# A written order for the whole first phase of a packed-attention and mixer kernel, with some copies moved from ScalarE to VectorE

## The chip, the cores and the metric

The kernel runs on one core of a Trainium2 chip. The metric is the device time of one execution in microseconds (us). Several runs of a kernel are summed up by their median. The engines are TensorE (PE in the profile; its weight loads are PEld), VectorE (DVE), ScalarE (ACT), GpSimd (POOL) and SyncE (SP), which here issues nearly all transfers.

## What is computed

The input has 8 batches of 8 heads; q, k and v are 576 x 64 per head, p is 32 x 64.

```python
    p_packed = sm_attn(p, k, v)
    out = sm_attn(q, p_packed, p_packed)
...
    xt = x.transpose(0, 2, 1)
    h = xt @ U @ V
    u = x + h.transpose(0, 2, 1)
    ch = np.maximum(u @ w_ch1, 0.0) @ w_ch2
    return (u + ch).astype(np.float32)
```

`sm_attn` is softmax attention. The first attention packs 576 keys into 32 rows per head, the second spreads them over 576 tokens. Its output, 576 x 512 per batch, goes through a token mixer of rank 32 (U, V) and a channel mixer (512 to 2048 to 512, with a Relu). U, V and the two channel matrices are float64 and are turned into float32 on the chip.

## The kernel before

**Two phases.** The first phase does the packing attention of all 16 units (a unit is a batch and four of its heads), turns the first 12 of 16 pieces of `w1` into float32, prepares U and V, and carries batch 0 through the second attention and the token mixer. The second phase runs the channel mixer over 8 batches: `gemm1` (h_ps, 16 slices per batch) and `gemm2` (o), each product split into three in fp32r from a high and a low part. What is left of the first phase (the last products of units 14 and 15), the next batches' attention and the `w2` conversions are put between these products by hand.

**One unit of the first phase.** `a_load` and `a_load_v` fetch k (tile `kx`, 576 KB, three buffers) and v (`vt`, 576 KB in three transfers, three buffers). `a_turn` transposes k on PE into PSUM (`k_ps`), ten products in three groups, and copies it out (`kT`; lines 276 and 280 on ScalarE, 274 on VectorE for one copy per unit). `a_scores` makes the scores (`s_ps`, one buffer), `a_softmax` takes their maximum on VectorE (line 496) and the exponential on ScalarE (line 498, tile `e`). `a_turn_back` transposes `e` (`m_ps`, lines 295 and 297) and copies it out (`eT`, lines 507 and 510), `a_pack` multiplies it with v (line 526) and scales (`two`), `a_heads` transposes that (line 536) into `ppTa`, which for batches 1 to 7 goes through DRAM (`ppTd`).

**Weights.** `float32_of` takes one ScalarE instruction (lines 79 and 185) and three of VectorE (lines 80 to 82) for each piece of 128 x 512 float64. The raw pieces lie in `bits` and `bits2`, two buffers each, so a load waits for an earlier piece's last VectorE instruction.

**What sets the order.** For the first phase the code loops over the units; a few lists say what is done in each round: `turns` (pieces of `w1`) and `early` (steps of batch 0). Within that phase a scheduler of the language's tile layer puts each engine's instructions into an order, from a model of their times. The second phase is compiled as it is written (`manual_schedule`, line 613). On the chip every engine works through its own list in order, and an instruction whose input is late holds all those behind it on its engine; that goes for SP's transfers too.

Just ahead of the second phase the code starts the loads of batch 1's q (`steps.pop(0)()`, line 602, tile `x`) and of three pieces of `w2` (line 193), and converts the first of these.

Of the kernel before, what the change touches and what calls it, by code (L numbers as in the profile page):

```python
# [20 lines left out]
def packed_attention_mixer_kernel(  # L21
# [51 lines left out]
    def float32_of(x, t, raw, out=None, tested=False):  # L73


        low, high = raw[:, :, 0], raw[:, :, 1]
        out = x if out is None else out.bitcast(I32)
        if not tested:
            nc.scalar.activation(t, high.bitcast(F32), AF.Abs, scale=REBIAS)
        nc.vector.tensor_single_scalar(x, t.bitcast(I32), 3, op=ALU.logical_shift_left)  # L80
        nc.vector.scalar_tensor_tensor(x, high, SIGN, x, op0=ALU.bitwise_and, op1=ALU.bitwise_or)
        nc.vector.scalar_tensor_tensor(out, low, 29, x, op0=ALU.logical_shift_right, op1=ALU.bitwise_or)
        return out.bitcast(F32)
# [86 lines left out]
    order = list(numbered("c" + "".join(plan)))  # L170
# [10 lines left out]
    tests = {}  # L181

    def test_w1(n):
        tests[n] = conv_tile(F32)
        nc.scalar.activation(tests[n], bits["w1", n][:, :, 1].bitcast(F32), AF.Abs, scale=REBIAS)

    def convert_w1(n):
        x, c = chunks[n]
        float32_of(conv_tile(I32), tests.pop(n), bits.pop(("w1", n)), w1t[x][:, QW * c:QW * c + QW], tested=True)
# [13 lines left out]
    def split_w2(kt, x):  # L203
        hi, lo = w2_parts(kt)
        nc.scalar.copy(hi, x)
        nc.vector.tensor_tensor(lo, x, hi.bitcast(F32), op=ALU.subtract)

# [10 lines left out]
    def load_uv():  # L218
        ub = x_tile()[:, :10 * R].bitcast(I32)
# [4 lines left out]
        vbits = x_tile()[:, :S // 2].bitcast(I32)  # L224
        nc.sync.dma_start(out=vbits, in_=V.rearrange("r (q x) -> (r q) x", q=4))
        return ub, vbits

    def prepare_uv(ub, vbits):
        ux = float32_of(conv_tile(I32)[:, :5 * R], conv_tile(F32)[:, :5 * R], ub.rearrange("p (x t) -> p x t", t=2))
        for (n, ks) in ((P, slice(0, 4)), (64, slice(4, 5))):  # L230
            nk = ks.stop - ks.start
            src = ux.rearrange("p (k r) -> p k r", k=5)[:n, ks].unsqueeze(2).to_broadcast([n, nk, 4, R])
            nc.vector.tensor_copy(ua4[:n, ks], src)
            nc.vector.tensor_tensor(ua4[:n, ks, 1], src[:, :, 0], ua4[:n, ks, 0].bitcast(F32), op=ALU.subtract)
        n = I // 2
        w = S // 4
        vq = float32_of(conv_tile(I32)[:, :w], conv_tile(F32)[:, :w], vbits.rearrange("p (x t) -> p x t", t=2))
        spread = x_tile()[:, :4 * P].rearrange("p (q a r) -> p q a r", q=4, a=4)
        nc.gpsimd.tensor_copy(spread, ident.rearrange("p (r q) -> p q r", q=4).unsqueeze(2).to_broadcast([P, 4, 4, R]))
        spread = spread.rearrange("p q a r -> p q (a r)")  # L240
        for hf in range(2):
            v_ps = bank()
            for y in range(2):
                nc.tensor.matmul(v_ps[:, w * y:w * y + w], lhsT=spread[:, 2 * hf + y], rhs=vq, start=True, stop=True)
            vx = v_ps[:, :2 * w].rearrange("p (i c) -> p i c", c=NT)
            blocks = vx[:, :, :8].rearrange("p i (a k r) -> p r k i a", a=2, k=2)
            ns = slice(n * hf, n * hf + n)
            pairs = [(vs[:, LAST][:, ns], vx[:, :, 8])]
            for r in range(2):
                dst = vs[:, HALF[r].start:HALF[r].start + 4 * I].rearrange("p (k i a) -> p k i a", k=2, a=2)[:, :, ns]  # L250
                pairs.append((dst, blocks[:, r]))
            for dst, src in pairs:
                nc.scalar.copy(dst, src)
                nc.vector.tensor_tensor(dst[96:], src[96:], dst[96:].bitcast(F32), op=ALU.subtract)


# [5 lines left out]
    def turn(t, x, h, bank, split=False):  # L262
# [3 lines left out]
        if h < 2:  # L266
# [3 lines left out]
            src = t_ps.rearrange("p (k a z i) -> p a z k i", k=2, a=2, z=2)  # L270
            for a in range(2):
                dst = t[:, 2 * h:2 * h + 2, :4 * I].rearrange("p z (k i a) -> p a z k i", k=2, a=2)[:, a]
                if a and split:
                    nc.vector.tensor_copy(dst, src[:, a])
                else:
                    nc.scalar.copy(dst, src[:, a])  # L276
        else:
            for h in range(2):
                nc.tensor.transpose(t_ps[:64, P * h:P * h + P], x[:, h, SM:], ident)
            nc.scalar.copy(t[:64, :, LAST], t_ps[:64, :2 * P].rearrange("p (h i) -> p h i", h=4))  # L280
# [21 lines left out]
    def attention(b, res):  # L302
# [11 lines left out]
        def turn_q(g, h):  # L314
            if h == 0:
                st["t", g] = pipe.tile([P, 4, 5 * I], F32, name="xT", bufs=1)
            turn(st["t", g], st["x", g], h, bank)

        def scores_q(g):
            e = st["e", g] = pipe.tile([P, S // 32, 32], F32, name="e", bufs=1)  # L320
            ss = [bank() for _ in range(2)]
# [515 lines left out]
```

## Time and profile before

| | us |
|---|---|
| median of 3 runs (823.89 to 826.15) | 824.42 |
| the profiled execution | 822.64 |
| its span in the profile | 820.9 |
| PE busy in the span | 802.2 (98%) |
| VectorE busy | 353.9 (43%) |
| ScalarE busy | 318.4 (39%) |
| GpSimd busy | 75.5 (9%) |
| transfers | 70.23 MB |

A busy PE is not a PE at its peak, since matmuls overlap and their ends are modelled. The shares are means over both phases. The profile's view by stretches gives the busy time of each engine between two times; the timeline lists instructions in order of time, with the idle time ahead of them and what ended it in brackets; the waits tell who waited for whom (us in total, times, the longest); a group of instructions stands with its count, its busy us and the mean ns of one. PEclk is the clock granted to TensorE as a share of full speed.

### The profile page before, as it was taken

What the parts mean: (1) busy time and instruction counts of PE and PEld (TensorE: products, weight loads), DVE (VectorE), ACT (ScalarE), POOL (GpSimd) and SP (SyncE); (2) the same over time, 40 slices, a digit from 0 to 9 for tenths busy, and PEclk for the clock granted to TensorE, in tenths of its full rate; (3) what the DMA queues carried; (4) which work ended last, traced back from release to release, by engine and by line L of the source; (5) the groups of instructions that cost most, each with busy time, mean ns of one, the idle gap of its engine ahead of it and who ended that gap; (6) DMA issues with size and microseconds to landing.
All of it is one profiled execution on the core that took longest, in us unless ns stands there. A gap on an engine that the chain in (4) does not pass through costs nothing.

```text
span 820.9 us, 15500 instructions
## 1 busy us (share of the span) xinstructions
PE 802.2 (98%) x6272; PEld 645.6 (79%) x6272; DVE 353.9 (43%) x782; ACT 318.4 (39%) x958; POOL 75.5 (9%) x108
## 2 busy tenths in 40 slices
PE   7889999999999999999999999999999999999997
PEld 5556677888888888887888888888888788888886
DVE  3777579973343234333434233333434234332231
ACT  4688765453333232343234232343234232332231
POOL 0122101110011001010101011000101011100000
PEclk8999999999999999999999999999999999999999
DMA  9999774325002120122002210131012200030001
GB/s 298 350 358 320 225 171 132 126 87 155 2 1 97 52 56 1 30 88 73 2 2 96 79 28 1 66 100 27 1 62 84 59 1 2 15 111 2 1 1 64
DMA packets 60310, 70.23 MB, mean 86 GB/s; under 512 B 22864, under 2 KB 41296, under 8 KB 60240
## 3 DMA queue, kind: packets, MB, share of 16 engines
q1 hardware_dynamic: 59920, 68.73, 27.2%
q8 instruction: 49, 0.80, 0.4%
q10 hardware_dynamic: 320, 0.52, 0.2%
q14 instruction: 21, 0.17, 0.1%
HBM read 53.64 MB, written 15.60 MB: 84 GB/s over the span
## 4 chain that ended last, share of the span: by engine, by line
PE 91%; DMA 4%; ACT 2%; DVE 1%; SPq 1%; issue 1%; POOL 0%; ACTq 0%; POOLq 0%
PE o L87 17%; PE o L89 16%; PE o L88 16%; PE h_ps L87 9%; PE h_ps L88 8%; PE h_ps L89 8%; PE t_ps L424 4%; DMA vt<-in_v_dram 2%; PE o L688 2%; PE t_ps L269 2%; DMA kx<-in_k_dram 2%; PE t_ps L289 1%; PE t_ps L367 1%; PE t_ps L295 1%; PE k_ps L269 1%; DMA bits<-in_moe_w_ch_dram 1%
## 5 line engine op out<-in xcount | busy, mean ns | idle before, releaser
L87 PE MATMUL o<-w2h,hh 128*128 128x512 f32 x512 | 206.5, 403 | 0.0
L89 PE MATMUL o<-w2h,hl 128*128 128x512 f32 x512 | 202.4, 395 | 0.0
L88 PE MATMUL o<-w2l,hh 128*128 128x512 f32 x512 | 201.9, 394 | 0.0
L671 DVE SCALAR_TENSOR_TENSOR hl<-h_ps,hh 128x256 fp32r<-128x256 f32 x256 | 105.4, 423 | 199.4 <-ACT hj L670 185.2
L668 ACT ACTIVATE hh<-h_ps 128x256 fp32r<-128x256 f32 x256 | 98.8, 387 | 179.5 <-PE h_ps L89 178.9
L87 PE MATMUL h_ps<-ah,wth 128*128 128x320 f32 (+1 forms) x512 | 157.7, 308 | 0.3 <-DVE hl L671 0.3
L88 PE MATMUL h_ps<-al,wth 128*128 128x320 f32 (+1 forms) x512 | 151.8, 296 | 0.1
L89 PE MATMUL h_ps<-ah,wtl 128*128 128x320 f32 (+1 forms) x512 | 151.4, 296 | 0.0
L87 PEld LDWEIGHTS h_ps<-ah,wth 128*128 128x128 f32 x512 | 96.6, 189 | 25.4 <-issue 20.2
L89 PEld LDWEIGHTS o<-w2h,hl 128*128 128x128 f32 x512 | 96.4, 188 | 22.4
L87 PEld LDWEIGHTS o<-w2h,hh 128*128 128x128 f32 x512 | 96.9, 189 | 21.0 <-issue 4.6
L88 PEld LDWEIGHTS o<-w2l,hh 128*128 128x128 f32 x512 | 97.0, 189 | 16.9
L88 PEld LDWEIGHTS h_ps<-al,wth 128*128 128x128 f32 x512 | 96.8, 189 | 2.4 <-POOL al L387 0.5
L89 PEld LDWEIGHTS h_ps<-ah,wtl 128*128 128x128 f32 x512 | 97.0, 189 | 0.0
L431 DVE TENSOR_TENSOR wtl<-t_ps,wth 128x256 fp32r<-128x256 f32 x128 | 48.5, 419 | 98.6 <-ACT wth L430 95.1
L430 ACT CAST wth<-t_ps 128x256 fp32r<-128x256 f32 x128 | 43.6, 374 | 105.5 <-PE t_ps L424 96.1
L387 POOL TENSOR_TENSOR al<-aT,ah 128x320 fp32r<-128x320 f32 (+1 forms) x32 | 25.7, 806 | 211.3 <-ACT ah L386 211.3
L330 POOL TENSOR_TENSOR e<-e,m 128x576 f32<-128x576 f32 x16 | 18.7, 1170 | 259.2 <-DVE m L329 255.1
L424 PE MATMUL t_ps<-w1t,ppT 64*32 64x512 f32 x512 | 35.9, 601 | 0.0
L276 ACT COPY xT<-t_ps 128x256 f32<-128x256 f32 x64 | 21.3, 392 | 37.5 <-PE t_ps L269 36.7
L386 ACT CAST ah<-aT 128x320 fp32r<-128x320 f32 (+1 forms) x32 | 13.7, 434 | 45.8 <-DVE aT L385 45.7
L670 ACT ACTIVATE hj<-h_ps 128x64 f32<-128x64 f32 x128 | 28.2, 220 | 0.0
(121 smaller groups left out, 824.5 us busy)
## 6 DMA issues: line engine op xcount, KB each, us to landing
bits<-in_moe_w_ch_dram SPq DMA_DIRECT2D x32, 512.0 KB, 4.6
kx<-in_k_dram SPq DMA_DIRECT2D x16, 576.0 KB, 7.0
x<-in_q_dram SPq DMA_DIRECT2D x16, 576.0 KB, 4.9
vt<-in_v_dram SPq DMA_DIRECT2D x32, 256.0 KB, 7.1
out_dram<-bits SPq DMA_DIRECT2D x32, 256.0 KB, 2.4
aD<-aT SPq DMA_DIRECT2D x16, 288.0 KB, 2.1
aP<-aD SPq DMA_DIRECT2D x32, 128.0 KB, 3.6
ppP<-ppD SPq DMA_DIRECT2D x32, 64.0 KB, 3.3
```

The costliest lines, as they stand in the source:

```text
L87: nc.tensor.matmul(ps, lhsT=lh, rhs=rh, start=start, stop=False)
L88: nc.tensor.matmul(ps, lhsT=lh, rhs=rl, start=False, stop=False)
L89: nc.tensor.matmul(ps, lhsT=ll, rhs=rh, start=False, stop=stop)
L269: nc.tensor.transpose(t_ps[:, o:o + P], x[:, h, P * j:P * j + P], ident)
L276: nc.scalar.copy(dst, src[:, a])
L387: nc.gpsimd.tensor_tensor(al[:, g, ns], aT[:, ns], ah[:, g, ns].bitcast(F32), op=ALU.subtract)
L424: nc.tensor.matmul(f_ps[g][xs], lhsT=ppT[b][zs, g, xs], rhs=w1t[h // 2][zs, QW * c:QW * c + QW], start=True, stop=True)
L430: nc.scalar.copy(hi[:, g], f_ps[g][:, cs])
L431: nc.vector.tensor_tensor(lo[:, g], f_ps[g][:, cs], hi[:, g].bitcast(F32), op=ALU.subtract)
L668: nc.scalar.activation(hh[:, ms], src, AF.Relu)
L670: nc.scalar.activation(hj[:, jslot(self.b, kt), self.js], h_ps[:, LAST], AF.Relu)
L671: nc.vector.scalar_tensor_tensor(hl[:, ms], src, 0.0, hh[:, ms].bitcast(F32), op0=ALU.max, op1=ALU.subtract)
```

## The change

The loop over the units is gone. In its place stands a string, `opening`, of 557 words. Each word is one group of instructions of one engine (or one load): `lk` loads k of the next unit, `k0` to `k2` are the three groups of transposes, `k0a` and the like the copies out of them, `s0` to `s2` scores, maximum and exponential, `b0` and `b1` the transposes back, `m0` to `m2` the packing, `h0` to `h2` the heads, `w0` to `w4` one piece of `w1`, `u` and `v` with a digit U and V, `q`, `s3` to `sa`, `t`, `x` and `y` batch 0, `f` the first folded weights, `z` the first piece of `w2`, `qq` the load of batch 1's q. The functions are cut up so that each word has one of its own. `manual_schedule` now begins ahead of this string, so each engine's list in the first phase is the string's order. A `v` at the end of a word (`k1bv`) gives that copy to VectorE instead of ScalarE; 61 words have it. The groups are those of before, with twelve pieces of `w1`, and the second phase's code does what it did.

```diff
-    turns = [0, 0, 1, 1, 0, 2, 0, 2, 1, 0, 2, 1, 0, 2, 0, 0]
-    early = [0, 0, 0, 0, 3, 2, 4, 3, 2, 5, 3, 2, 0, 0, 0, 0]
-    NW1 = sum(turns)
+    opening = (
+        "w0 lk lp lp lv u0 w1 w2 lk w3 lk lv w4 p0 k1 p1 p0 lv k1av k1bv k2 p1v k0 k2av u1 k0bv lk u2 k0av lp u2 s0 "
...
+        "h0 m1 b1a h1v m2 z5 z0 z6 "
+    )
+    NW1 = opening.split().count("w0")
...
+    def copy(scalar):
+        return nc.scalar.copy if scalar else nc.vector.tensor_copy
...
-            for a in range(2):
-                dst = t[:, 2 * h:2 * h + 2, :4 * I].rearrange("p z (k i a) -> p a z k i", k=2, a=2)[:, a]
-                if a and split:
-                    nc.vector.tensor_copy(dst, src[:, a])
-                else:
-                    nc.scalar.copy(dst, src[:, a])
...
+    def turned(t, t_ps, h, a, scalar=True):
+        if h < 2:
+            src = t_ps.rearrange("p (k a z i) -> p a z k i", k=2, a=2, z=2)
+            dst = t[:, 2 * h:2 * h + 2, :4 * I].rearrange("p z (k i a) -> p a z k i", k=2, a=2)[:, a]
+            copy(scalar)(dst, src[:, a])
+        else:
+            copy(scalar)(t[:64, :, LAST], t_ps[:64, :2 * P].rearrange("p (h i) -> p h i", h=4))
...
+    ctx.enter_context(tc.manual_schedule())
...
-    n_w1 = 0
-    for i in range(NU):
-        if i > 0:
-            a_turn_back(i - 1, bank_a("m"))
-        a_scores(i)
-        if i + 1 < NU:
-            a_load_v(i + 1)
-            a_turn(i + 1)
-        if i + 2 < NU:
-            a_load(i + 2)
-        a_softmax(i)
...
+    for word in opening.split():
+        name = word.rstrip("v") if word not in stages else word
+        stage = next(stages[name])
+        if name in either:
+            stage(name == word)
+        else:
+            stage()
...
-    ctx.enter_context(tc.manual_schedule())
```

**SP, near the end of the first phase.** `kx` is k, `vt` is v, `x` is batch 1's q, `bits` from `in_moe_w_ch_dram` with line 193 is `w2`. Before, from the load of the second piece of `w2` on; the last pair of `vt` is unit 13's:

```order
L193 DMA bits<-in_moe_w_ch_dram 128x1024
L542 DMA ppTd_80<-ppTa 128x256
L193 DMA bits<-in_moe_w_ch_dram 128x1024
L258 DMA x<-in_q_dram 128x2x576
L258 DMA kx<-in_k_dram 128x2x576
L465 DMA vt<-in_v_dram 64x4x256 x2
L467 DMA vt<-in_v_dram 64x4x64
L258 DMA x<-in_q_dram 128x2x576
L465 DMA vt<-in_v_dram 64x4x256 x2
L467 DMA vt<-in_v_dram 64x4x64
```

The same place in the changed kernel, from the load of the last k on; line 220 is now the load of `w2`, lines 622 and 624 that of v, line 311 that of k and q. Units 12, 13 and 14 are the three `vt`:

```order
L311 DMA kx<-in_k_dram 128x2x576
L622 DMA vt<-in_v_dram 64x4x256 x2
L624 DMA vt<-in_v_dram 64x4x64
L220 DMA bits<-in_moe_w_ch_dram 128x1024
L622 DMA vt<-in_v_dram 64x4x256 x2
L624 DMA vt<-in_v_dram 64x4x64
L723 DMA ppTd_81<-ppTa 128x256
L622 DMA vt<-in_v_dram 64x4x256 x2
L624 DMA vt<-in_v_dram 64x4x64
L311 DMA x<-in_q_dram 128x2x576 x2
L129 DMA ppT<-ppTd_78 128x256
L220 DMA bits<-in_moe_w_ch_dram 128x1024
```

Both q loads, the load of `ppT` and two of the three `w2` loads have moved behind unit 13's v; one `w2` load, the first, stands ahead of it.

**VectorE, at the start of the program**, behind its first memset. `w1t` is a converted piece of `w1`, `os` the working tiles of a conversion, `x` the raw bits of U, `ua` the spread U, `sm` the first unit's maximum. Before:

```order
L274 COPY kT<-k_ps 128x2x128
L496 TENSOR_REDUCE sm<-s_ps 128x1
L80 TENSOR_SCALAR os<-os 128x512
L274 COPY kT<-k_ps 128x2x128
L81 SCALAR_TENSOR_TENSOR os<-bits_146,os 128x512
```

Now, from the second instruction of the first conversion to the first maximum:

```order
L81 SCALAR_TENSOR_TENSOR os<-bits_138,os 128x512
L82 SCALAR_TENSOR_TENSOR w1t_101<-bits_138,os 128x512
L332 COPY kT<-k_ps 128x2x128 x2
L638 TENSOR_SCALAR pT<-t_ps 128x256
L334 COPY kT<-k_ps 64x4x64
L332 COPY kT<-k_ps 128x2x128
L80 TENSOR_SCALAR os<-os 128x160
L332 COPY kT<-k_ps 128x2x128
L81 SCALAR_TENSOR_TENSOR os<-x,os 128x160
L82 SCALAR_TENSOR_TENSOR os<-x,os 128x160
L273 CAST ua_109<-os 128x512
L658 TENSOR_REDUCE sm<-s_ps 128x1
```

A whole conversion, five copies of `kT`, one of `pT` and the preparation of U now stand ahead of the first maximum, which was VectorE's second instruction there.

**VectorE, at the end of the first phase**, up to the second phase's first `hl`. Before:

```order
L496 TENSOR_REDUCE sm<-s_ps 128x1
L274 COPY kT<-k_ps 128x2x128
L514 RECIPROCAL sm<-sm 128x1
L496 TENSOR_REDUCE sm<-s_ps 128x1
L671 SCALAR_TENSOR_TENSOR hl<-h_ps_1710,hh 128x256
```

Now; `w2l` is the low part of the first piece of `w2`, `aT` batch 0's mixed tokens:

```order
L461 TENSOR_TENSOR aT_1312<-t_ps,aT_1312 128x256
L80 TENSOR_SCALAR os<-os 128x512
L658 TENSOR_REDUCE sm<-s_ps 128x1
L81 SCALAR_TENSOR_TENSOR os<-bits,os 128x512
L687 RECIPROCAL sm<-sm 128x1
L82 SCALAR_TENSOR_TENSOR os<-bits,os 128x512
L718 COPY ppTa<-t_ps 128x128
L239 TENSOR_TENSOR w2l_106<-os,w2h_105 128x512
L866 SCALAR_TENSOR_TENSOR hl<-h_ps_1710,hh 128x256
```

The conversion of the first piece of `w2` has moved from some twenty VectorE instructions earlier to the very end of the phase.

More of the change, by code (lines that the diff above doesn't have):

```diff
@@ L1 @@
 from contextlib import ExitStack
-from itertools import product
+from itertools import count, product
 import concourse.bass as bass
@@ L223, in load_uv, with load_v @@
         nc.sync.dma_start(out=ub[:64, 8 * R:], in_=rows[:, 8])
[L224 to L232, printed above, removed]
+    def load_v():
+        uv["vb"] = x_tile()[:, :S // 2].bitcast(I32)
+        nc.sync.dma_start(out=uv["vb"], in_=V.rearrange("r (q x) -> (r q) x", q=4))
@@ new lines, in step_turn, with step_scores, step_most, step_total @@
+        def step_turn(g, h):
+            turn_q(g, h)
+            for a in range(2 if h < 2 else 1):
+                turned_q(g, h, a)
+        def step_scores(g):
+            scores_q(g)
+            side(g, 0)
+            side(g, 1)
+        def step_most(g):
+            most(g)
+            each(g, "m", ALU.subtract)
+        def step_total(g):
+            for k in range(3):
+                total(g, k)
+            each(g, "s", ALU.mult)
+        def step_tokens(k0):
+            if k0 == 0:
+                room()
+            tokens(k0)
+            split_tokens(k0, False)
+            split_tokens(k0, True)
@@ L747, in convert_late_w1 @@
         n = order.pop(0)[1]
-        test_w1(n)
-        convert_w1(n)
+        begin_w1(n)
+        for _ in range(3):
+            go_w1(n)
         load_next()
```

514 lines of the change are left out of this document (316 added, 198 removed), and 16 rows, old and new, of the table opening.

## The prediction

> **What bounds the kernel now.** I read the page first, then the busy time by stretches, then the matrix engine's timeline for the end of the first phase.
>
> ```profile
> span 820.9 us, 15500 instructions
> ...
> 0.00:20.00 20.00, 15.40 (x109) 11.94 (x110) 5.78 (x11) 9.04 (x23) 1.45 (x11) 0.83 0.93 295
> 20.00:40.00 20.00, 17.11 (x293) 10.45 (x291) 14.26 (x36) 14.33 (x47) 2.46 (x4) 0.92 1.08 351
> 40.00:60.00 20.00, 18.29 (x302) 12.10 (x294) 14.38 (x28) 16.93 (x54) 4.62 (x8) 0.99 1.07 363
> 60.00:80.00 20.00, 17.23 (x269) 11.99 (x271) 16.55 (x34) 16.68 (x49) 3.37 (x5) 1.00 1.00 318
> 80.00:95.49 15.49, 14.80 (x300) 9.12 (x297) 7.44 (x17) 12.72 (x44) 3.87 (x7) 1.00 0.92 293
> 95.49:820.90 725.41, 719.32 (x5026) 590.05 (x5020) 295.51 (x659) 248.73 (x745) 59.74 (x73) 1.00 0.18 54
> ...
> 0.00:95.49 95.49, 82.84 (x1252) 55.58 (x1253) 58.42 (x123) 69.71 (x214) 15.76 (x35) 0.95 1.00 325
> ```
>
> After the stretch's length stand the busy us of PE, PEld, DVE (VectorE), ACT (ScalarE) and POOL, then the granted clock, the share of the DMA engines and GB/s. The row from 95.49 to 820.90 is the second phase: PE is busy for 719.32 of 725.41 us, so a change ahead of it counts by as much as it moves that phase's start. That start is the first h_ps product, at 95.49 us:
>
> ```profile
> 94.66 0.90 PE L526 MATMUL m_ps<-vt,eT 128*32 128x64 f32 x40
> 95.49 0.42 PE L87 MATMUL h_ps<-ah,wth 128*128 128x320 f32 x1
> ...
> 97.68 0.42 PE L87 MATMUL h_ps<-ah,wth 128*128 128x320 f32 x1 [0.33 <-DVE hl L671]
> ```
>
> Before it PE has two kinds of loss: 95.49 - 82.84 = 12.65 us idle, and a clock under full speed. The waits of that time, longest first, are for the softmax chain and for copies out of PSUM:
>
> ```profile
> PE m_ps L295 <- ACT e L498: 5.0, 6, 2.9
> PE m_ps L526 <- ACT eT L507: 1.9, 2, 1.1
> PE t_ps L536 <- DVE e L323: 1.5, 1, 1.5
> ```
>
> The DMA engines have a share of 1.00 over the same 95.49 us: transfers are the second limit there, not a spare resource.
>
> **The change, part by part.** No work is added to or taken from the first phase; PE ends it with the same pieces. Three things move.
>
> *Transfers.* In the old order two loads of w2 (`bits`, L193) and both q loads of batch 1 go out ahead of the load of v for unit 13, the last that the phase needs:
>
> ```profile
> 73.93 0.54 SPq L193 DMA_DIRECT2D bits<-in_moe_w_ch_dram  x1
> 76.26 0.38 SPq L193 DMA_DIRECT2D bits<-in_moe_w_ch_dram  x1
> 76.82 0.38 SPq L258 DMA_DIRECT2D x<-in_q_dram  x1
> 77.52 0.38 SPq L258 DMA_DIRECT2D kx<-in_k_dram  x1
> ...
> 80.26 0.81 SPq L258 DMA_DIRECT2D x<-in_q_dram  x1
> 81.17 1.26 SPq L465 DMA_DIRECT2D vt<-in_v_dram  x2
> ...
> bits<-in_moe_w_ch_dram SPq DMA_DIRECT2D x32, 512.0 KB, 4.6
> x<-in_q_dram SPq DMA_DIRECT2D x16, 576.0 KB, 4.9
> vt<-in_v_dram SPq DMA_DIRECT2D x32, 256.0 KB, 7.1
> ...
> vt<-in_v_dram SPq DMA_DIRECT2D x16, 64.0 KB, 6.7
> ```
>
> In the new order they stand behind it. Moved past it: 2 x 0.52 + 2 x 0.59 MB and a 0.13 MB ppT load, 2.35 MB. Summed over the queue (sixteen k, fourteen v of 0.59 MB with their tail, twelve w1 of 0.52 MB, and the small ones), 29.3 MB go out up to that v before, 26.9 MB after. At the pace of the rows 5.90 + 7.02 + 7.26 + 6.36 = 26.5 MB are through at 80 us, so v of unit 13 is in at about 81 us; if the stretch 60:80 ran at the 357 GB/s of the two before it, at 79. Behind it PE has only the products of that unit and a few transposes, 1.2 us. The transfers alone would let the phase end at **82.2 us**. SP issues in order, so each of these loads also holds what follows it: v of unit 15 waits for unit 12's products to free a `vt` buffer, and the third w2 load stands behind it and behind the first w2's conversion, whose buffer it takes. Nothing that the first phase needs is queued behind those two.
>
> *VectorE.* 61 copies carry the mark that gives them to VectorE, which makes 16 already (row L274): 45 move, 28 of 256 columns, 3 of 512, 14 of 64 or 128 columns.
>
> ```profile
> L276 ACT COPY kT<-k_ps 128x256 f32<-128x256 f32 x48 | 16.4, 401 | 3.8 <-PE k_ps L269 3.7
> L507 ACT COPY eT<-m_ps 128x512 f32<-128x512 f32 x15 | 8.9, 595 | 1.4 <-PE m_ps L295 1.2
> L510 ACT COPY eT<-m_ps 64x128 f32<-64x128 f32 x15 | 4.0, 268 | 0.4 <-PE m_ps L297 0.4
> ...
> L81 DVE SCALAR_TENSOR_TENSOR os<-bits,os 128x512 int32<-128x512 int32 x13 | 10.4, 798 | 0.1
> L82 DVE SCALAR_TENSOR_TENSOR w1t<-bits,os 128x512 int32<-128x512 int32 x12 | 8.1, 677 | 0.2
> L274 DVE COPY kT<-k_ps 128x256 f32<-128x256 f32 x16 | 6.7, 419 | 16.5 <-ACT kT L276 16.4
> ...
> L233 DVE CAST ua<-os 128x512 fp32r<-128x512 f32 x1 | 1.4, 1427 | 0.0
> ...
> 60.80 0.43 DVE L274 COPY kT<-k_ps 128x256 f32<-128x256 f32 x1
> 61.14 0.52 DVE L323 STREAM_TRANSPOSE e<-t_ps 128x320 f32<-128x320 f32 x1
> ```
>
> On VectorE: 28 x 0.419 + 3 x 0.677 (its nearest 512-column row, between 0.595 and 0.798) + 14 x 0.268 (ScalarE's row, none of VectorE's own) = 17.5 us, less the overlap of neighbours (the copy at 60.80 takes 0.43 but the next starts after 0.34): 45 x 0.08 = 3.6, so 13.9 us. VectorE's work in the phase grows from 58.42 to 72.3 us; ScalarE's falls by about as much, from 69.71 to some 57. It has work from about 5 us on (the first w1 piece is then in). At the share of its best stretch, 16.55 of 20 us or 83%, it is done at 5 + 87.1 = 92.1 us; at 90%, at 85.3; the middle is **88.7 us**.
>
> *PE.* After 20 us it has 82.84 - 15.40 = 67.4 us of work, 66.0 at full clock (0.08 x 17.11 off). In its best stretch, 80:95.49, it was busy 14.80 of 15.49 us, 95.5%. At that share it ends at 20 + 69.1 = **89.1 us**, with the first 20 us as they were. I add 0.5 us there, since w1 now goes out ahead of the first k: at 295 GB/s that is 1.8 us at most, and the twelve idle products on zeros cover part of it. If all of it shows, 90.9.
>
> The latest of the three is PE's, **89.6 us**, 5.9 earlier. At the phase's end the first w2 conversion now stands on VectorE and ScalarE directly ahead of `hl` and `hh`; PE waits there 0.33 us already, and I put 0.4 more on it. If the last exponential and that chain add up worse, it is 1.5 us; below nothing it can't be. The later w2 loads must also be in when ScalarE wants them, about 2 us into the second phase: 29.5 MB, at 88.5 us by the same pace. With a start at 89.6 this is covered; with one before 86 the transfer holds ScalarE's queue, the next Relu behind it, and then PE. So gains over 10 us are mostly given back.
>
> The sum against the profiled execution: 822.64 (span 820.9 and 1.74 around it) - 5.9 + 0.4 = 817.1 us. The median of the runs shown is 1.78 above that execution, so **818.9 us**.
>
> *A rule on the start.* The stretch that holds the 2.9 us wait for `e` ran at a granted clock of 0.66, the first maximum began at 10.57 us, and the first k's products at 6.96:
>
> ```profile
> 10.00:20.00 10.00, 7.11 (x63) 4.74 (x48) 5.20 (x9) 5.86 (x17) 0.00 (x0) 0.66 1.08 346
> ...
> 6.96 1.09 PE L269 MATMUL k_ps<-ident,kx 128*128 128x128 f32 x8
> ...
> 10.57 0.76 DVE L496 TENSOR_REDUCE sm<-s_ps 128x1 f32<-128x576 f32 x1 [1.52 <-PE s_ps L289]
> ```
>
> The Trainium skill, "TensorE: Matmul & The Clock Gate", section "Why this matters for your kernels", says that PE gaps of more than about 3 us send the clock back to half speed. The row agrees so far, and the rule speaks against an order whose first softmax comes later; rival two is that case, worked out from the rows. At the rule's half clock instead of the row's 0.66, rival two would come to 823.2 us.
>
> **The rivals.**
> One, *PE follows the loads without a gap*, and the transfers bind. For it: DMA shares of 1.07 and 1.08 from 20 to 60 us, so more loads ahead of PE is all that can help there. Against it: PE at 100% after 20 us still ends at 86.0, and a start at 85.5 needs half a microsecond more out of the first 20, where it idles 4.6. That is 10 us, less 0.4 at the phase's end and 0.6 at the w2 loads: -9, **815.4 us**. Chance 0.17.
>
> Two, *the start falls behind*. In the new order VectorE makes pT and the five copies of the first unit, three U operations and the 1.43 us cast ahead of its first maximum. From 6.96 + 1.8 us on, 2.0 for the copies, 0.9 for U (three of about 0.3) and 1.4 give 13.0, 2.4 us later than the 10.57 of now; PE then does its next 2.4 us of work at 0.66, 1.2 us more. Of these 3.6 us my sum holds 0.5: -5.5 + 3.1, **822.0 us**. Against it: PE has products of units 1 and 2 to put into that gap. Chance 0.12.
>
> Three, *VectorE becomes the late engine*, slower. It decides at 72.3 / (95.1 - 5) = 80% busy: below that the phase ends later than now. After 20 us it was busy for 70% (52.6 of 75.5), ScalarE for 80%. At 76% it is done at 100.1 us: +4.6 and 0.4 at the end, **829.4 us**. For it: VectorE works strictly in its written order, and a maximum late by one load holds every copy behind it. Against it: 16.4 us of its idle time were waits for ScalarE's copy of the same tile, which mostly go. Chance 0.12.
>
> Four, *nothing shows*: other gaps of the same size arise, **824.4 us**. Chance 0.06.
>
> **How the numbers follow.** My forecast has 0.53: a first phase that ends at 86.5 to 92.5 us, 816 to 822. A measurement of this kernel tells about 0.3% from no change, 2.5 us, so 822 is the edge of faster; rival two lies on it and is halved. Faster: 0.53 + 0.17 + 0.06 = 0.76; same: 0.06 + 0.06 = 0.12; slower: 0.12. The range goes from 814, which leaves out the better third of rival one (0.06), to 827, which leaves out most of rival three (0.10).
>
> **What would show it.** The first h_ps product at 88 to 91 us; PE over 90% busy and VectorE 80 to 90% busy after 20 us; the load of v for unit 13 issued before 78 us; no PE wait over 1 us in the first 10 us of the second phase; the second phase's length within 1 us of 725.4. Wrong: VectorE under 80% busy, a first maximum after 14 us with a clock under 0.8 at 10:20, or a second phase that is longer by more than 2 us.

## The result and the profile after

| | us |
|---|---|
| before, median of 4 runs (823.89 to 826.15) | 825.16 |
| after, median of 4 runs (813.55 to 814.61) | 813.68 |
| ratio, with its 95% interval | 0.9864 (0.9846 to 0.9882) |
| after, the profiled execution | 813.64 |
| its span | 811.8 |

After is 11.5 us faster, where 5 to 6 were forecast; the time lies just under the forecast's range. In a later comparison it was 814.69 against 823.16 (ratio 0.9891, 0.9874 to 0.9908), 8.5 us, and that time lies just inside the range. The profiled executions differ by 9.0 (822.64 and 813.64). So 2 to 3 of the 11.5 us are the spread from one comparison to the next (2.0 in before's median, 1.0 in after's), and some 9 are the change.

The busy time by stretches, in the columns of the prediction's first fence. The second phase begins at 87.39 us:

```profile
0.00:20.00 20.00, 15.34 (x171) 11.75 (x171) 10.73 (x29) 6.77 (x15) 2.75 (x12) 1.00 0.95 297
20.00:40.00 20.00, 16.68 (x288) 10.63 (x273) 16.38 (x44) 13.87 (x42) 1.17 (x4) 1.00 1.07 363
40.00:60.00 20.00, 19.03 (x354) 13.40 (x353) 17.21 (x40) 15.92 (x47) 4.45 (x8) 1.00 1.03 341
60.00:80.00 20.00, 18.67 (x322) 12.84 (x319) 18.80 (x41) 16.05 (x46) 4.04 (x6) 1.00 1.08 343
80.00:87.39 7.39, 7.26 (x142) 4.83 (x141) 7.21 (x16) 7.14 (x23) 3.64 (x5) 1.00 1.03 331
87.39:811.80 724.41, 716.74 (x5022) 588.24 (x5021) 296.85 (x664) 248.46 (x745) 59.91 (x74) 1.00 0.19 56
...
0.00:87.39 87.39, 76.98 (x1252) 53.45 (x1253) 70.33 (x165) 59.75 (x168) 16.04 (x35) 1.00 1.03 336
...
20.00:87.39 67.39, 61.63 (x1097) 41.70 (x1082) 59.60 (x138) 52.98 (x154) 13.29 (x23) 1.00 1.06 347
```

Three things differ from before. The granted clock is 1.00 in every stretch, where before had 0.83, 0.92 and 0.99 in the first three. In the first 20 us PE is busy for the same 15.3 us, but does 171 products and not 109. From 60 us on the transfers run at 343 and 331 GB/s, not at 318 and 293. Over the whole phase PE is busy for 5.9 us less (76.98 against 82.84, with 1252 products in both) and idle for 2.2 less (10.41 against 12.65). In the profile of the later comparison the second phase of after begins at 88.49 us, 1.1 later, again with 171 products in the first 20 us and a clock of 1.00; so the place of that start is known to about 1 us.

PE's timeline at the end of the first phase, and the row that stands for the 0.33 us wait for `hl` of before:

```profile
86.03 1.26 PE L699 MATMUL m_ps<-vt,eT 128*32 128x64 f32 x40
87.23 0.30 PE L351 MATMUL m_ps<-ident,e 128*64 128x128 f32 x1
87.36 0.27 PE L712 MATMUL t_ps<-ident,two 128*128 128x128 f32 x1
87.39 0.40 PE L95 MATMUL h_ps<-ah,wth 128*128 128x320 f32 x1
...
89.92 0.42 PE L95 MATMUL h_ps<-ah,wth 128*128 128x320 f32 x1 [0.69 <-DVE hl L866]
```

The waits of PE in the first phase, in all, times, longest. The 5.0 us for `e` have become 1.2 + 1.2, with none over 1.8:

```profile
PE k_ps L322 <- DVE kT L334: 2.2, 2, 1.8
PE s_ps L343 <- DVE kT L332: 1.5, 2, 1.1
PE m_ps L349 <- ACT e L663: 1.2, 1, 1.2
PE s_ps L343 <- ACT e L663: 1.2, 1, 1.2
PE t_ps L751 <- DVE os L748: 1.1, 1, 1.1
PE t_ps L629 <- DMA pn<-in_p_dram: 1.0, 1, 1.0
```

### The profile page after: what moved, and what is told of

It reads as the page before. It is cut to its first block, busy times and chain, and to the rows that moved or that the text cites. A ratio compares the mean times of both kernels' runs of the same rounds, so it can differ in the third digit from the quotient of the medians.

```text
span 811.8 us, 15483 instructions
## 1 busy us (share of the span) xinstructions
PE 793.7 (98%) x6272; PEld 641.7 (79%) x6272; DVE 367.2 (45%) x827; ACT 308.2 (38%) x913; POOL 76.0 (9%) x108
## 4 chain that ended last, share of the span: by engine, by line
PE 92%; DVE 2%; DMA 1%; ACT 1%; issue 1%; SPq 0%; ACTq 0%; DVEq 0%
PE o L95 16%; PE o L97 16%; PE o L96 16%; PE h_ps L95 9%; PE h_ps L97 8%; PE h_ps L96 8%; PE t_ps L572 4%; PE o L883 2%; PE t_ps L322 2%; DMA x<-in_q_dram 1%; PE t_ps L343 1%; PE k_ps L322 1%; PE t_ps L436 1%; PE t_ps L349 1%; PE m_ps L699 1%; PE s_ps L343 1%
## 5 line engine op out<-in xcount | busy, mean ns | idle before, releaser
L583 ACT CAST wth<-t_ps 128x256 fp32r<-128x256 f32 x128 | 43.4, 374 | 104.8 <-PE t_ps L572 95.5
```

What stands on the lines that cost most here:

```text
L583: nc.scalar.copy(hi[:, g], src)
```

## The experiments

Before's order comes out of the scheduler and stands nowhere in the code, so no single step of it can be moved by hand. Most experiments therefore use after's code with another string. "Written before" is a string of the same 557 words in the order in which the trace of before shows the first instruction of each group, with before's 16 copies on VectorE. Kernels of different comparisons are set side by side by their ratio to before; for after that is 0.9891, from its repeat (experiment 8).

**1. Written before.**

```diff
-        "w0 lk lp lp lv u0 w1 w2 lk w3 lk lv w4 p0 k1 p1 p0 lv k1av k1bv k2 p1v k0 k2av u1 k0bv lk u2 k0av lp u2 s0 "
+        "lp lk lk lv w0 w0 lv p0 k0 p1 k1 k0a lp k0b k1a k2 k1bv k2a lk k0 w0 s0 k0a k0b k1 s1 k2 lv w1 k1a w2 k1bv "
...
```

> The code of after with a string of 557 words that writes down the order in which before ran its first phase (each word put where the trace of before shows the first instruction of its group), and before's choice of engine for every copy. The theory that the order and the choice of engine are all that counts: 824 to 826 us, the first h_ps product at 95 to 96 us, TensorE's clock halved at 13 to 20 us as in before. The rival that the writing in whole groups costs or pays by itself (before's scheduler mixed the products of neighbouring groups): off by over 1 us, to either side. It is the base of the three other kernels, so that what they show can be set against it one edit at a time.

Measured: 825.53 us (ratio 1.0026, 1.0017 to 1.0036), start of the second phase at 97.77. The order is reproduced, but PE's first long wait is 3.65 us in this trace (2.89 in before), the clock then falls for less time (0.91 in the first 20 us, 0.83 in before), and there is a new stall. PE, GpSimd and ScalarE at the stall, one after the other:

```profile
58.57 0.95 PE L348 MATMUL m_ps<-ident,e 128*128 128x128 f32 x4 [3.65 <-ACT e L662]
```

```profile
54.98 0.31 POOL L412 MEMSET x<- 64x256 f32 x1 [6.28 <-PE t_ps L324]
55.38 1.16 POOL L391 TENSOR_TENSOR e<-e,m 128x576 f32<-128x576 f32 x1
```

```profile
56.56 0.68 ACT L394 ACTIVATE e<-e 128x576 f32<-128x576 f32 x1 [2.46 <-POOL e L391]
57.15 0.64 ACT L79 ACTIVATE os<-bits 128x512 f32<-128x512 f32 x1
57.70 0.72 ACT L662 ACTIVATE e<-s_ps,sm 128x576 f32<-128x576 f32 x1
```

A memset on GpSimd waits for an `x` buffer, the subtraction behind it waits, batch 0's exponential on ScalarE waits for that, and unit 7's exponential, whose maximum was done at 54.5 us, stands third in ScalarE's queue. PE then waits 3.65 us for it. The cause is one word, `t0`, which the string has too early.

**2. Written before, mended.** `t0` goes 26 words later:

```diff
-m2 w1 t0 q2a w2 s3 s1 k0 w3 s2 k1 s4 lk k0a b0 s4 k0b w4 w1 b1 s0 s5 k1a w0 b0a h0 q0 w2 b1a s6 h1 k1bv
+m2 w1 q2a w2 s3 s1 k0 w3 s2 k1 s4 lk k0a b0 s4 k0b w4 w1 b1 s0 s5 k1a w0 b0a h0 q0 w2 b1a s6 t0 h1 k1bv
```

> The first written order of before ran 2.1 us behind before, and its trace shows one place for it: the word t0 (two memsets on GpSimd, each waiting for an x buffer) stood ahead of s6 (the subtraction of the maxima for q), so that s6 began at 55.38 us and not at 52.14, the exponential of the eighth unit stood behind s7 on ScalarE, and TensorE waited 3.65 us for it. Here t0 stands right behind the first s6, nothing else is moved. Expected: 2 to 3 us faster than the first written order, level with before within 0.7 us, first h_ps at 95 to 96 us.

Measured: 822.34 us (0.9988, 0.9976 to 0.9999), start at 94.64; 3.2 us from the move of one word. This is the base for the rest, a thousandth under before.

**3. The copies alone**, on the first string: each copy goes to the engine that it has in after, 61 to VectorE for 16.

```diff
-lp lk lk lv w0 w0 lv p0 k0 p1 k1 k0a lp k0b k1a k2 k1bv k2a lk k0 w0 s0 k0a k0b k1
+lp lk lk lv w0 w0 lv p0 k0 p1 k1 k0av lp k0bv k1av k2 k1bv k2av lk k0 w0 s0 k0av k0b k1
...
```

> Before's written order with after's choice of engine for the copies (61 on VectorE where before had 16), no word moved. Theory (the order at the start is what pays; the copies pay only together with it): 0.5 to 3 us faster than the written order of before, and the clock still falls at 13 us. Rival (moving copies off ScalarE is the gain, since TensorE waited 5.0 us for e and VectorE 16.4 us for kT behind ScalarE): 6 us or more faster. Third way (VectorE, with an order made for fewer copies, becomes late): slower by 1 us or more.

Measured: 828.21 us (1.0059, 1.0043 to 1.0075), 2.7 us slower than its base. This is the third way, VectorE late: ScalarE's waits for VectorE's maximum rose from 3.8 to 8.1 us, and it waited 4.3 us for VectorE's copies of `kT`, where its base shows no such wait. PE's waits for `e` rose from 9.7 to 10.5 us in all and it waited 1.8 us for loads of k; these do not add up to the whole 2.7, and the rest was not followed.

**4. The later loads alone**, on the first string:

```diff
-t3 k0 z0 z3 k1 k0a
+t3 k0 z3 k1 k0a
...
-s2 h2 k1bv z0 z5 qq r0 z6 k2 x1
+s2 h2 k1bv z5 r0 z6 k2 x1
...
-k2 k1bv y2 y3 p0 k2a lv h0 y3 p1
+k2 k1bv y2 y3 p0 k2a lv qq z0 z0 h0 y3 p1
```

> Before's written order with the q loads and the second and third w2 load put behind the v load of unit 13, nothing else moved. The prediction counted on 2.35 MB fewer ahead of that load. If transfers bind the end of the first phase, some 3 us or more faster than the written order of before (2.35 MB at the 334 GB/s of before's rows is 7 us at most). If the queue position matters little because the v load also waits for its buffer, which the products of unit 10 free: within 1 us of it.

Measured: 824.88 us (1.0019, 1.0009 to 1.0028), start at 97.99 against 97.77. Nothing: the load of v for unit 13 went out at 83.35 us and not at 85.50, but PE waited for it in neither trace. In this order transfers do not bind the end.

**5. Fifteen idle products in the first gap**, first on the unmended string, then on the mended one:

```diff
+    def fill(n):
+        f_ps = bank()
+        for _ in range(15):
+            nc.tensor.matmul(f_ps[:, :P], lhsT=ident, rhs=ident, start=True, stop=True)
...
-k0b k1 s1 k2 lv w1 k1a
+k0b k1 s1 k2 g0 lv w1 k1a
```

> Before's written order with 15 more TensorE products (ident by ident, 128x128 f32, into a bank that nothing reads) right behind the last transposes ahead of the 2.89 us gap at 11 to 14 us. Theory of the clock (the gap cost the half clock that follows it): the clock stays 1.00 up to 20 us, the third unit's scores begin 2 us or more earlier than in the written order of before, and the second phase begins 1.5 to 3.4 us earlier. Rival (TensorE would wait for loads or copies later anyway): the clock stays full and the start of the second phase moves by less than 0.7 us. Second rival (the gap isn't what halves the clock): the clock falls all the same.

> The same 15 idle products in the gap at 11 to 14 us, now on the mended written order. In the first try they kept the clock at 1.00 up to 20 us, brought the eighth unit's scores 0.86 us forward, and the stall at 55 us swallowed that. Theory of the clock: with that stall gone, the second phase begins 0.8 to 2 us ahead of the mended order without them. Rival: later waits swallow any early lead, 0 +- 0.5 us.

Measured: 825.24 us (1.0014, 1.0002 to 1.0025) and 822.81 (0.9988, 0.9979 to 0.9997); 0.3 less and 0.5 more than without. The second phase begins at 98.11 us (97.77 without) and at 96.12 (94.64). The stretches of the mended string:

```profile
0.00:20.00 20.00, 15.41 (x109) 11.94 (x110) 5.76 (x11) 9.09 (x23) 1.44 (x11) 0.83 0.93 296
20.00:40.00 20.00, 16.41 (x294) 10.65 (x293) 14.20 (x35) 13.91 (x46) 2.37 (x4) 0.92 1.06 357
40.00:60.00 20.00, 17.35 (x294) 11.79 (x292) 14.70 (x29) 17.21 (x55) 4.68 (x8) 0.99 1.06 351
```

and with the idle products, then PE where their lead was lost:

```profile
0.00:20.00 20.00, 16.77 (x186) 13.66 (x193) 6.24 (x13) 10.55 (x27) 1.44 (x11) 1.00 0.92 291
20.00:40.00 20.00, 16.52 (x263) 11.03 (x262) 13.73 (x33) 12.59 (x40) 2.37 (x4) 0.91 1.07 356
40.00:60.00 20.00, 16.39 (x261) 11.87 (x269) 13.22 (x26) 16.79 (x53) 4.43 (x7) 0.91 1.07 355
```

```profile
21.54 1.92 PE L321 MATMUL k_ps<-ident,kx 128*128 128x128 f32 x8 [0.78 <-DMA kx<-in_k_dram]
...
26.17 0.76 PE L342 MATMUL s_ps<-kT,pT 64*32 64x320 f32 x16
```

The clock is full up to 20 us and the third unit's scores come at 19.93 us, not 21.93. Then PE waits for the fourth k, the clock falls there (eight transposes take 1.92 us, not 1.09), and the fourth unit's scores start at 26.17 us, as without (26.20). So the rival is borne out in that nothing is gained: in before's order the early lead is swallowed, by a load and by the next fall of the clock.

**6. Crosses of the two orders.** Cross A takes after's words up to the third unit's scores (76 words, 20 us) and then all others in before's order; cross B takes before's 74 words up to there and then after's order.

> A cross of both orders: after's words (and engines of copies) up to the third unit's scores, that is 76 words or the first 20 us, then all other words in before's order with before's engines. It gives the early lead of after (third unit's scores at 19.6 us instead of 22.0, clock full). If an early lead is kept, 2.4 to 5 us faster than the mended written order. If later waits (loads, buffers) swallow it: within 0.7 us of it. If the two pieces don't fit together (words that before had done by then now come late): slower.

> The other cross: before's words and engines up to the third unit's scores (74 words), then all others in after's order with after's engines. If the gain lies in the later 67 us (fewer and shorter waits of TensorE there), 5 us or more faster than the mended written order, near after (813.7) plus 2 to 3 us. If the gain lies in the first 20 us: less than 4 us faster.

Measured: 824.96 us (1.0017, 1.0008 to 1.0027) and 825.02 (1.0022, 1.0007 to 1.0036), 2.6 and 2.7 slower than written before, mended. Each has one stall at its seam. Cross A, ScalarE and PE:

```profile
24.69 0.66 ACT L79 ACTIVATE os<-bits 128x512 f32<-128x512 f32 x1 [3.65 <-DMA bits<-in_moe_w_ch_dram]
```

```profile
25.88 0.42 PE L350 MATMUL m_ps<-ident,e 128*64 128x128 f32 x1 [5.43 <-ACT eT L674]
```

Cross B the same with U's conversion:

```profile
25.15 0.34 ACT L79 ACTIVATE os<-x 128x160 f32<-128x160 f32 x1 [4.01 <-DMA x<-in_moe_U_dram]
```

```profile
29.30 0.61 PE L324 MATMUL k_ps<-ident,kx 128*64 128x128 f32 x2 [6.05 <-DVE kT L331]
```

A conversion stands ahead of its load, and copies that have nothing to do with it stand behind it. The order of after is right only for the times at which its own loads land. So the seams were mended: in cross A one conversion of `w1`, the start of the next and a load go behind the fourth unit's exponential; in cross B first U's conversion goes there, and, when that had only uncovered V's (5.64 us on ScalarE, 3.55 on PE), the loads of U and V go to the start instead.

```diff
-lk k0av s0 w1 w2 w3 w0 w4 w0 b1 w1 r1 b0a b1a w0 m1 m2
+lk k0av s0 w0 w0 b1 r1 b0a b1a m1 m2
...
-k2 v1 lk k1bv s2 lk
+k2 v1 lk k1bv s2 w1 w2 w3 w4 w1 w0 lk
...
-m0 w0 s0 u1 u2 u2 lp u2 u3 u3 u3 u3 lv k0
+m0 w0 s0 lp lv k0
...
-lp lk lk lv w0 w0 lv p0
+lp lk lk lv w0 w0 u0 v0 lv p0
```

The first two pieces are cross A's, the third and the fourth are cross B's first and second mend.

> The first cross again (after's first 76 words, then before's order), mended at its seam: there ScalarE stood 3.65 us at a w1 conversion whose load hadn't landed, and TensorE 5.43 us behind it. Two w1 conversions and one w1 load now stand behind the exponential of the fourth unit. If after's first 20 us are worth something on before's later order: 2 to 4 us faster than the mended written order of before (ratio 0.994 to 0.997). If not: the same as it (0.998 to 1.000).

> The second cross again (before's first 74 words, then after's order), mended at its seam: there ScalarE stood 4.01 us at the conversion of U, whose load before issues at 17 us, and TensorE 6.05 us behind it. U's conversion now stands behind the exponential of the fourth unit. From the fourth unit's scores to the second phase after's words took 59.1 us in the first cross as in after (59.7), before's words 67 to 69. If that holds, with those scores at about 28 us: start at 87 to 89 us, 814 to 817 us (ratio 0.988 to 0.992). If the short second part was only owed to loads that had run ahead during the stall: 819 us or more.

> The second cross once more: before's first 74 words, then after's order. In both earlier tries ScalarE stood at a conversion whose load hadn't landed (U: 4.01 us, then V: 5.64 us), because before's piece issues these two loads at 18 to 21 us. Here both loads stand behind the second w1 load, at the start; nothing else is moved. If after's order behind that point gains by itself: fourth unit's scores at 27 to 30 us, second phase from 86 to 90 us, ratio 0.987 to 0.993. If it gains only together with after's first 20 us: ratio 0.996 or above.

Measured: cross A mended 821.06 us (0.9973, 0.9962 to 0.9983); cross B with U's conversion moved 824.36 (1.0012, 0.9998 to 1.0027), with the early loads 818.90 (0.9941, 0.9924 to 0.9959). The stretch up to the fourth unit's scores, and from there to the second phase. After:

```profile
0.00:27.65 27.65, 22.66 (x291) 16.91 (x291) 17.23 (x48) 12.77 (x34) 3.22 (x14) 1.00 0.98 319
27.65:87.39 59.74, 54.31 (x962) 36.54 (x962) 53.10 (x118) 46.98 (x134) 12.82 (x21) 1.00 1.05 343
```

Written before, mended:

```profile
0.00:26.20 26.20, 20.57 (x197) 15.47 (x197) 7.44 (x15) 13.96 (x38) 1.68 (x12) 0.87 0.96 315
26.20:94.64 68.44, 59.76 (x1057) 39.74 (x1056) 51.01 (x108) 55.48 (x178) 14.03 (x23) 0.98 1.01 326
```

Cross A, mended:

```profile
0.00:23.90 23.90, 18.41 (x196) 13.51 (x197) 11.73 (x31) 10.01 (x25) 2.74 (x13) 1.00 0.98 309
23.90:92.98 69.08, 59.88 (x1058) 39.98 (x1057) 50.38 (x104) 56.42 (x177) 12.35 (x22) 0.98 1.03 336
```

Cross B with the early loads:

```profile
0.00:34.09 34.09, 26.96 (x291) 20.09 (x292) 15.06 (x39) 15.96 (x45) 3.24 (x14) 0.85 0.98 320
34.09:93.40 59.31, 54.30 (x962) 36.43 (x962) 52.70 (x117) 46.51 (x134) 12.83 (x21) 1.00 0.96 311
```

The second rows go by the order: 59.3 to 59.7 us with after's words, 68.4 to 69.1 with before's, whatever came ahead (with the first form of each cross, before itself and after's repeat, 59.1 to 60.6 and 67.0 to 69.3). The first rows tell that this is not all gain: after has 95 more products behind it when the fourth unit's scores begin (291 against 196 or 197), at 54.31 / 962 = 0.056 us each some 5.4 us of PE. Of the 9 us between the second rows, 5.4 are work done earlier and the rest a faster pace.

Set against written before (0.9988), after's beginning on before's continuation is worth 0.0015, 1.2 us; after's continuation on before's beginning 0.0047, 3.9 us; both together 0.0097, 8.0 us (each to 1.3 to 1.7 us, by the intervals, so the 1.2 is not clear of nothing). Both crosses lie between the two cases expected of them. The beginning is worth 4.1 us (give or take 2.0) if after's continuation follows (0.9941 to 0.9891) and 1.2 if before's does. In cross B's first stretch PE is busy for 26.96 us where after's needs 22.66 for the same 291 products, at a clock of 0.85 and not 1.00. That is 4.3 us of lower clock, and the second row shows that the continuation did not take them up. Not all of it belongs to before's first 20 us: at the seam PE still waited 1.79 us for a copy of `kT` that stood behind U's conversion on VectorE, and behind that the clock fell once more (0.83, 0.50 and 0.81 in the two-us stretches from 26 to 32 us). So cross B puts the worth of after's beginning too high rather than too low.

**7. Parts of the change taken out of after.** Its copies back on before's engines, 16 on VectorE for 61 (`k1av` becomes `k1a` and so on); its v loads of units 13 and 14 behind the q loads and the second `w2` load; its string left to the scheduler:

```diff
-k0 k2av u1 k0bv lk u2 k0av
+k0 k2a u1 k0b lk u2 k0a
...
-b1a k2 m1 lv s1 t1
+b1a k2 m1 s1 t1
...
-h0 m1 lv x0 b1a
+h0 m1 x0 b1a
...
-s0 y1 z0 b1a
+s0 y1 z0 lv lv b1a
...
-    ctx.enter_context(tc.manual_schedule())
     zeros = conv_tile(F32)[:, :P]
...
     actx.close()
+    ctx.enter_context(tc.manual_schedule())
```

> After's written order, no word moved, with 45 of its 61 VectorE copies given back to ScalarE, as before had them. The copies alone on before's written order cost 3.3 us. If order and engines belong together (VectorE takes copies just where ScalarE stands on something else), 3 to 8 us slower than after. If the order alone makes the gain: within 1 us of after's 813.7.

> After with the v loads of units 13 and 14 put behind the q loads and the second w2 load: the transfer part of the change undone. On before's order the same move in the other direction gave nothing (within 1 us). The prediction's term (transfers ahead of that load bind the end): 3 us or more slower than after. The theory that the order of the steps makes the gain: less than 1.5 us slower.

> After's 61 copies on VectorE, its finer steps and its string as the order in which the steps are stated, but the scheduler that before used decides what each engine issues next. If what pays is the order that the string fixes on each engine: at least half of the 11.5 us is lost, 819 us or more. If the engines of the copies and the order of stating pay: within 2 us of after's 813.7.

Measured: copies back 817.41 us (0.9928, 0.9905 to 0.9952), 2.7 to 3.0 slower than after; loads back 818.79 (0.9945, 0.9926 to 0.9964), 4.1 to 4.4 slower; scheduler 823.50 (1.0003, 0.9993 to 1.0013), all of the gain gone, though the copies, the finer steps and the order in which they are stated are after's. With the copies back PE's waits for `e` come to 5.3 us (4.1 and 1.2) where after has 2.4. With the loads back PE goes as in after up to the last units (the scores of the last unit at 84.78 us, 84.65 in after) and then waits for v of unit 13, which SP issued at 82.33 us and not at 74.40. SP's queue, then PE:

```profile
74.57 0.38 SPq L722 DMA_DIRECT2D ppTd<-ppTa  x1
80.19 0.89 SPq L310 DMA_DIRECT2D x<-in_q_dram  x2
...
82.33 1.51 SPq L621 DMA_DIRECT2D vt<-in_v_dram  x2
```

```profile
90.91 1.49 PE L698 MATMUL m_ps<-vt,eT 128*32 128x64 f32 x40 [4.78 <-DMA vt<-in_v_dram]
```

From 74.95 to 80.19 us the two q loads ahead of it waited for their `x` buffers and held the queue, and from 78 to 82 us the transfers ran at no more than 163 and 60 GB/s. So these 4 us are at least in part a place in SP's queue behind loads that can't go yet, and not the bytes that the prediction counted; the run doesn't separate the two.

So the same two parts that gave nothing, or a loss, on before's order cost 4 and 3 us when they are missing from after's.

**8. After once more, and three tries to beat it.** The first try puts two copies of `kT`'s last columns back on ScalarE; the second does that and puts k and p ahead of `w1` at the start; the third does the first and puts the transposes of k ahead of the products with p:

```diff
-w1 v6 k2av s2 k2av lp k1
+w1 v6 k2a s2 k2a lp k1
...
-w0 lk lp lp lv u0
+lk lp lp w0 lv u0
...
-w4 p0 k1 p1 p0
+w4 k1 p0 p1 p0
```

> After once more, unchanged, beside before on the same chip as the three kernels here. Before's median was 825.16 in the comparison that gave the result and 823.4 to 823.6 in three later ones. If the difference is what the two profiled executions show (span shorter by 9.1 us): a ratio of 0.988 to 0.990. If the 11.5 us stands: 0.986 or below.

> After with two of its VectorE copies (the last columns of kT of the fifth and sixth unit) back on ScalarE: one of them ended TensorE's longest wait of after's first phase, 1.79 us at 29 to 31 us, behind other VectorE work. If each wait of TensorE is paid in full at the end of the phase: 1 to 2 us faster than after. If later waits take up what is gained early, as they took up the filler's lead: within 0.5 us of after.

> After with the first k and both first p loads ahead of the first w1 load (TensorE's first wait, for pn, was 0.99 to 2.06 us in the traces of after's order), and with the two copies of kT's last columns on ScalarE. If early time is kept to the end: 1 to 2.5 us faster than after. If it is taken up later: within 0.5 us of after.

> After with TensorE's first two groups exchanged (the first transposes of k ahead of the products with p, whose load it waited 0.99 to 2.06 us for, while k's load is issued ahead of p's) and the last columns of kT of the fifth and sixth unit copied by ScalarE. If k has landed by then, VectorE's copies of kT and with them the first scores come up to 1.1 us earlier, and since after's order carried a delay of 5.3 us at the fourth unit to the end as 4.9 (the kernel with k and p ahead of w1), 1 to 2 us faster than after's 814.7. If k lands with p: within 0.7 us of it.

Measured: after 814.69 us (0.9891, 0.9874 to 0.9908); the two copies 814.39 (0.9891, 0.9869 to 0.9913), no difference; k and p first 818.46 (0.9935, 0.9918 to 0.9952), 3.8 slower; transposes of k first 814.06 (0.9881, 0.9862 to 0.9900), within the interval of after. None beats it. The slow one shows the queue again, on ScalarE, VectorE and PE:

```profile
8.51 0.66 ACT L79 ACTIVATE os<-bits 128x512 f32<-128x512 f32 x1 [6.48 <-DMA bits<-in_moe_w_ch_dram]
```

```profile
11.00 0.75 DVE L331 COPY kT<-k_ps 128x256 f32<-128x256 f32 x2
```

```profile
11.90 0.63 PE L321 MATMUL k_ps<-ident,kx 128*128 128x128 f32 x4 [3.61 <-DVE kT L331]
```

The `w1` load came later, its conversion still stands first on ScalarE and VectorE, so the copies of k came at 11.00 us and not at 8.59. Its clock was 0.81 in the first 20 us. Of the 5.3 us by which its fourth unit's scores were behind after's (32.96 against 27.65), 4.9 were left at the start of the second phase (92.30 against 87.39); against after's second profile (27.88 and 88.49) it is 3.8 of 5.1. After's order has little slack.

## Why the prediction was wrong in its size

Of the 5.2 us between 818.9 and 813.68, 2.2 are the start of the second phase (87.39 against 89.6), 1.4 the second phase itself, 1.7 the step from the profiled execution to the median; 0.1 more around the span goes the other way. By after's second profile the start is only 1.1 us early (88.49).

**What bounds the kernel.** Right. PE is busy for 716.74 of 724.41 us of the second phase, and the profiled executions differ by 9.0 us where the starts differ by 8.1.

**Transfers.** The v load of unit 13 went out at 74.40 us, before 78 as forecast, and taking that part out of after costs 4.1 to 4.4 us, by a wait for just the load that the prediction named. But the prediction reckoned in bytes at the pace of the rows; in that run the queue stood still for 5.2 us behind q loads without a buffer, which the prediction had only as a remark ("SP issues in order"). That the part counts only together with the rest (nothing on written before) it did not say.

**VectorE.** Right. 72.3 us of work were forecast, 70.33 came; it was busy for 59.60 of 67.39 us, 88%, within the 83 to 90% of the sum, and the phase ended 1.3 us ahead of the 88.7 at which it was to be done.

**PE, the step that failed:** "At that share it ends at 20 + 69.1 = 89.1 us, with the first 20 us as they were." They were not. PE did 62 products more in them, at a clock of 1.00 and not 0.83, and 61.63 us of work were left, not 66.0: at the step's own 95.5% that is 64.5 us instead of 69.1, 4.6 earlier. The share was too high: 61.63 / 67.39 = 91.5%, 2.9 later. The added 0.5 was in fact inside the first 20 us (the first product on data began at 7.31 us, 0.35 after before's 6.96). -4.6 + 2.9 - 0.5 = -2.2. The two errors partly cancel, and that was luck. After's second profile tells the same: 61.40 us of work left, 89.6% busy, -4.8 + 4.2 - 0.5 = -1.1. The change there was on record, since the order shows what VectorE does ahead of the first maximum, but the prediction used it only for rival two, as a loss. Cross B shows what the step left out, with the seam's stall added: with before's first 20 us, after's continuation starts the second phase at 93.40 us.

**The phase's end.** 0.4 us was put on the chain ahead of `hl`; the wait grew from 0.33 to 0.69 in after's first profile and was 0.35 in its second. The size is right, or a little high.

**The second phase.** Forecast unchanged but for that 0.4; it was 1.0 us shorter. In the eighteen profiles of the experiments, span less start goes from 722.9 to 726.0 us, so a single profile does not settle this, and it stays open. (The lowest is that of the scheduler on after's steps, whose second phase began at 98.42 us.)

**The step to the median.** The profile of before was one of its quicker executions, and the prediction carried its 1.78 us over to after. After's profiled execution and median are 813.64 and 813.68. Before's median was 823.16 to 823.91 in the five later comparisons, only 0.5 to 1.3 over its profiled execution.

**The rivals.** One (no gap for PE, the transfers bind, 815.4) is nearest in time, but not as it was put: PE still idled 5.8 us after 20 us, and at the end PE, VectorE and ScalarE are all nearly full (7.26, 7.21 and 7.14 of 7.39 us), while PE waits for no load there; it does only once the transfer part is undone. Two (the start falls behind): the first maximum came at 12.07 us, 1.5 later than before, but PE had other products there, its wait was 1.20 us instead of 2.89, and the clock stayed full. Three (VectorE late) did not come; on written before, the copies alone did make it slower, by 2.7 us. Four (nothing shows) is what the scheduler gives with the same parts: 823.50.

**The rule on the start.** The clock did fall in before at a gap of 2.89 us, and did not in after, whose longest gap is 1.79. The Trainium skill, "TensorE: Matmul & The Clock Gate", section "Why this matters for your kernels", sets the limit at gaps of about 3 us. The traces agree as to direction, but a gap need not be that long: with the idle products the clock fell behind gaps of 1.08 and 0.78 us at 18 to 22 us. Nor does the length of a gap settle it. With the copies alone (experiment 3) a gap of 2.82 us ahead of 13.76 us left the clock at 1.00 up to 22 us, and in the first written order the gap of 3.65 us was followed by about 3.4 us at half clock (0.60 and 0.54 in the two-us stretches from 14 to 18 us), where the 2.88 us of the mended one was followed by about 6.8 (0.73, 0.50, 0.50 and 0.56 from 12 to 20).

## What to carry to other kernels

When several engines each work through a fixed list, price a new order by how much work each engine has behind it at a few points in time, the beginning among them, and not by a share of the old profile for the rest. A part of such a change can be worth nothing alone and several us in its place, so test it by taking it out of the new order as well as by putting it into the old one. An instruction whose load or buffer may be late belongs behind those that don't need it: the long stalls that were followed here came from a short conversion, a memset, or a load without a free buffer, in front of others.

## What the runs showed of the hardware

**What a short fall of the clock costs depends on the order behind it.** In before the granted clock of two-us stretches is 0.75, 0.50, 0.50 and 0.54 from 12 to 20 us, and 0.73, 0.50 and 0.92 from 36 to 42: about 6.8 and 3.4 us at half clock. Removing the first fall saved nothing in before's order (experiment 5). In cross B, with two falls ahead of after's continuation, PE was busy for 4.3 us more, and the second phase began 4.9 to 6.0 us later than in after's two profiles.

**VectorE beside GpSimd.** The cast of U took 1427 ns in before, and the prediction put that at the start of after. There it took 427. In before it began during a GpSimd copy and ended 0.3 us after it; in after it began first. GpSimd and VectorE of before, then of after:

```profile
29.17 1.49 POOL L239 COPY x<-ident 128x512 f32<-128x512 f32 x1 [6.16 <-ACT kT L280]
```

```profile
29.52 1.60 DVE L233 CAST ua<-os 128x512 fp32r<-128x512 f32 x2
```

```profile
11.70 0.43 DVE L273 CAST ua<-os 128x512 fp32r<-128x512 f32 x1
12.07 0.76 DVE L658 TENSOR_REDUCE sm<-s_ps 128x1 f32<-128x576 f32 x1
```

```profile
11.78 1.31 POOL L286 COPY x<-ident 128x512 f32<-128x512 f32 x1 [9.61 <-DVE os L82]
```

The Trainium skill, "SBUF — State Buffer", section "SBUF: two separate sides", says that a GpSimd instruction and a VectorE instruction of certain kinds (in a mode that takes two ports, or with two SBUF inputs) share a pair of ports, which one of them holds for its whole length while the other waits. The traces agree: the later of the two paid. GpSimd's copy began 0.08 us behind the cast in after and took 1.31 us; in cross A, mended, where no cast ran beside it, it took 1.12. So a duration from one order may hold another engine's work; that 1.0 us was in rival two's price.
